# The last 64 keys of two head pairs as four 64x64 products in the array's quarters, with the work re-timed

## The chip, the cores and the metric

The kernel runs on one core of a Trainium2 chip. The metric is device time in microseconds (us) of one execution. Five engines work side by side: PE (TensorE, matmuls), ACT (ScalarE), DVE (VectorE), POOL (GpSimd, unused here but for constants) and SP (SyncE, which issues all DMAs). PE has a 128x128 array; a matmul that uses 64 of its rows or 64 of its columns leaves the other half to a second one.

## The reference

Batch 4, 12 heads, 448 positions, head size 64, model width 768, inner width 1024, all in float32.

```python
scores = scale * q @ k.T                 # per head, 448 x 448
scores = cap * tanh(scores / cap)
attn = exp(scores - max); attn /= sum(attn) + 1e-9
x = attn @ v                             # heads side by side: 448 x 768 per batch
h = relu(x @ w_in)                       # 448 x 1024
c = conv_w[0]*h[s-1] + conv_w[1]*h[s] + conv_w[2]*h[s+1]
out = (h * sigmoid(c)) @ w_out           # 448 x 768
```

## The kernel before

Heads are worked in pairs: 24 pairs p, six to a batch; the two heads of a pair stand in the lower and upper 64 partitions of `qr` and `kr`. The 448 keys of a pair are three units u of 128 keys and a rest of 64 (NU = 3, KF = 384).

**Scores** (`scores`, L420): for a unit, two matmuls with 64 contraction rows, one for each head, run side by side in the two row halves of the array, into the two banks of a PSUM tile `sp` (two such tiles, 128 x 2 x 448). The rest of both heads is one 128x128 matmul: the host lays the last 64 keys of head 0 and head 1 out in 128 columns with zeros between (`layout`, L824), so the tile `spr` has head 0 in partitions 0 to 63 and head 1 above. Pairs 0 to 11 (RAW) multiply in plain float32, which PE does in two records for each matmul; pairs 12 to 23 split q and k into a high and a low part (`qs`, `ks`, made by DVE and ACT) and use three float32r passes. ACT then does tanh and exp on each tile: on 896 columns for a unit, on 448 for the rest, into `E`.

**Values** (`values`, L463): for each of the four units, two float32 matmuls of 128 rows and 64 columns, side by side in the two column halves, add into `acc`. From pair 1 on (BUNDLE) all eight stand in one piece.

**Sums**: pairs 0 to 3 sum `E` on PE against ones (`sm`, four matmuls of 32 columns side by side). From pair 4 on DVE adds the units into a tile `P` (`add`, L489), adds the rest in two instructions on 64 partitions (`add_rest`, L497 or L494), and PE sums `P`. The reciprocals, `xu` (scaled output), and its split into `x` (high, low) follow.

**Feed forward** (`feed_forward`, L650), once a batch: `hps` (8 blocks f of 18 float32r passes), relu, three taps and the sigmoid by groups of f (0 to 2, 3 to 5, 6 and 7), the product split into `gh` and `gl`, then `ops`, 6 blocks e of 24 passes. `w_in` and `w_out` come as float64 and are decoded by ACT and DVE (`st_i`, `st_o`); the decoded `w_out` is written to DRAM (`wo`) and read back as `wh`, `wl` for each block.

The **order** on every engine comes from `Plan.run` (L85), a list planner: of the tasks that can start it takes the one with the earliest due time, counting its own costs for each engine and 0.19 us for a change of PE mode (`full`, `row`, `col`, `quad`). Due times follow from FIRST, STEP (us per pair) and DUE. The engines wait for each other by semaphores alone, so real durations set the times.

Of the kernel before, what the change touches and what calls it, by code (L numbers as in the profile page):

```python
# [20 lines left out]
TWO = 12  # L21
RAW = tuple(range(12))
STEP = (9.5,) * 8 + (17.2,) * 16
FIRST = 6.0
DUE = {"w_in": (4.4, 57.93), "w_out": (63.06, 84.72), "prep": -5.0, "load": -34.0, "av": 5.0, "sum": 4.0,
       "x": 14.0, "x0": 14.0, "one": 4.5, "rec": 2.0, "ff": 27.0, "gate": -25.0, "wq": 6.0, "wld": -15.0}
# [146 lines left out]
def capped_attention_gated_mlp_kernel(  # L173
# [17 lines left out]
    KW = KF + 128  # L191
# [183 lines left out]
    prep, b_in, t_v, b_v = {}, {}, {}, {}  # L375
# [5 lines left out]
    def prepare(p):  # L381
        b, j = divmod(p, NPB)
        t0 = when(p)
        bq, bk, bs = Buf("q"), Buf("k"), Buf("s")
        b_v[p] = Buf("v")
        ld = t0 + DUE["load"] if p else -97
        lk = dma("sp", 128 * KW * 4, lambda: new(p, raw_p, "kr", [128, KW]), lambda: k[b, j], ld, (), [bk],
                 after=t0 - AHEAD["qk"])
        lq = dma("sp", 128 * S * 4, lambda: new(p, raw_p, "qr", [128, S]), lambda: q[b, j], ld, (), [bq],
                 after=t0 - AHEAD["qk"])  # L390
        t_v[p] = dma("sp", 128 * KW * 4, lambda: new(p, raw_p, "vr", [128, KW], bufs=BUFS["v"]), lambda: v[b, j], ld + 3, (),
                     [b_v[p]], after=t0 - AHEAD["v"])
        if p in RAW:
            prep[p], b_in[p] = [lk, lq], [bq, bk]
# [12 lines left out]

        def k_hi(eng):
            copy(eng, new(p, raw_p, "ks", [128, 2, KW], F32R, bufs=BUFS["s"])[:, 0], T[p]["kr"])

        def k_lo():
            sub(T[p]["ks"][:, 1], T[p]["kr"], f32(T[p]["ks"][:, 0]))
# [3 lines left out]
        c = either(KW, k_hi, due + 0.1, [lk, a], uses=[bk, bs])  # L416
        c2 = task("dve", dve(KW), k_lo, due + 0.4, [c], uses=[bk, bs])
        prep[p], b_in[p] = [a, a2, c, c2], [bs]

    def scores(units, due):  # L420

        rest = units[0][1] == NU
        n = 1 if rest else 2
        out = [{} for _ in units]
        bufs = [Buf("m" if rest else "sp") for _ in units]

        def qk():
            for (p, u), sp in zip(units, out):
                if rest:
                    sp[0] = ps_m.tile([128, 512], F32, tag="m", name="spr").rearrange("p (a s) -> p a s", a=1)  # L430
                else:
                    sp[0] = ps_s.tile([128, 2, 512], F32, tag="sp", name="sp")
                X = T[p]
                if p in RAW:
                    parts = [(X["kr"], X["qr"])]
                else:
                    parts = [(X["ks"][:, w], X["qs"][:, l]) for w, l in ((0, 0), (0, 1), (1, 0))]
                for i, (w, x) in enumerate(parts):
                    for h in range(n):
                        r = slice(0, 128) if rest else half[h]  # L440
                        nc.tensor.matmul(out=sp[0][:, h, 0:S], lhsT=w[r, 128 * u:128 * u + 128], rhs=x[r],  # L441
                                         start=i == 0, stop=i == len(parts) - 1)

        cost = sum(2 * HALF if p in RAW else 3 * PASS for p, u in units)
        t_qk = task("pe", cost, qk, due, [t for p, u in units for t in prep[p]], bufs,
                    [b for p, u in units for b in b_in[p]], mode="full" if rest else "row")
        for (p, u), sp, bsp in zip(units, out, bufs):
            t_u = when(p, u / (NU + 1))
            raw = p in RAW
            b_e[p, u] = Buf("e")  # L450

            def tanh(sp=sp, raw=raw):
                x = sp[0][:, 0:n, 0:S]
                nc.scalar.activation(out=x, in_=x, func=ACTF.Tanh, **({"scale": tsc_sb[:, 0:1]} if raw else {}))  # L454

            def exp(p=p, u=u, sp=sp):
                E[p, u] = e_p.tile([128, 2, S], F32, tag="e", name="E")
                nc.scalar.activation(out=E[p, u][:, 0:n], in_=sp[0][:, 0:n, 0:S], func=ACTF.Exp, scale=cap_sb[:, 0:1])  # L458

            t = task("act", act(n * S, True, ptr=raw), tanh, t_u + 1, [t_qk, t_tsc], uses=[bsp])  # L460
            t_exp[p, u] = task("act", act(n * S, True, ptr=True), exp, t_u + 2, [t], [b_e[p, u]], [bsp], table="exp")

    def values(p):  # L463

        b_acc[p] = Buf("acc")

        def av(us):
            if us[0] == 0:
                T[p]["acc"] = ps_a.tile([128, 512], F32, tag="acc", name="acc")
            for u in us:  # L470
                for h in range(2):
                    c = 128 * u + 64 * h
                    nc.tensor.matmul(out=T[p]["acc"][half[h], 0:S], lhsT=T[p]["vr"][:, c:c + 64],  # L473
                                     rhs=E[p, u][:, 0 if u == NU else h, :], start=u == 0, stop=u == NU)

        for us in ([range(NU + 1)] if p >= BUNDLE else [[u] for u in range(NU + 1)]):
            t_av[p] = task("pe", 2 * HALF * len(us), lambda us=us: av(us), when(p, us[-1] / (NU + 1)) + DUE["av"],
                           [t_exp[p, u] for u in us] + [t_v[p]] + ([t_av[p]] if us[0] else []), [] if us[0] else [b_acc[p]],
                           ([b_acc[p]] if us[0] else []) + [b_v[p]] + [b_e[p, u] for u in us], mode="col")
# [3 lines left out]

# [19 lines left out]
        t_P[p] = [task("dve", dve(S), lambda h=h: add_rest(h), when(p, 0.75) + 3.5 + h, t + [t_exp[p, NU], t_eps_key],
                       uses=[b_P[p], b_e[p, NU]]) for h in range(2)]
# [273 lines left out]
    units = [(p, u) for p in range(NP) for u in range(NU)]  # L778
    while units:
        n = 2 if units[0][0] >= TWO and len(units) > 1 else 1  # L780
        scores(units[:n], when(units[0][0], units[0][1] / (NU + 1)))
        units = units[n:]
    for p in range(NP):
        scores([(p, NU)], when(p, NU / (NU + 1)))
# [15 lines left out]
def layout(inputs):  # L800
# [57 lines left out]
```

## Time and profile before

| | us |
|---|---|
| three runs | 434.56, 434.90, 435.56 |
| median | 434.9 |
| span of the profiled execution, first to last instruction | 432.9 |
| PE busy, share of the span | 418.6, 97% |
| DVE busy | 309.9, 72% |
| ACT busy | 289.1, 67% |

The page gives the profiled execution its span and no other time; the median lies 2.0 us above it, for what is around the first and the last instruction. Busy times are unions of intervals, and a matmul's interval overlaps the next one's: what a matmul costs in a stream is read from start to start. The granted clock of TensorE is at its upper level (1.00 of 2.4 GHz) in every stretch.

### The profile page before, as it was taken

The numbers are of one execution on the slowest core, as the hardware profiler recorded it, in microseconds if no ns is written. First come the engines' busy times: TensorE is split into PE (matmuls) and PEld (weight loads), VectorE is DVE, ScalarE is ACT, GpSimd is POOL, SyncE is SP. The second block draws the span as 40 slices with busy tenths as digits, with TensorE's granted clock in tenths as the row PEclk, the third lists the DMA queues.
The fourth block names the chain that finished last, engine by engine and source line by source line (L and its number), as shares of the span: only waits on it lengthen the run. The fifth ranks groups of instructions, "written<-read, shape, count | busy, mean of one in ns | idle before, by whom it ended". The sixth has DMA issues, their size and how long they took to land.

```text
span 432.9 us, 5890 instructions
## 1 busy us (share of the span) xinstructions
PE 418.6 (97%) x2106; PEld 288.1 (67%) x2106; DVE 309.9 (72%) x548; ACT 289.1 (67%) x412; POOL 0.2 (0%) x4
## 2 busy tenths in 40 slices
PE   7987889999999999999999999999999999999996
PEld 3222234457577676868667868668677787999995
DVE  1788899999999965589899773498899813166400
ACT  4999999988999665358888545368697811454411
POOL 0000000000000000000000000000000000000000
PEclk9999999999999999999999999999999999999999
DMA  7668557887556988650211762633000374500181
GB/s 273 217 225 263 182 181 234 274 244 254 206 161 200 345 292 263 229 210 5 70 28 44 224 225 90 202 130 120 24 2 0 131 251 148 183 0 2 30 336 53
DMA packets 37085, 70.90 MB, mean 164 GB/s; under 512 B 6336, under 2 KB 20160, under 8 KB 37056
## 3 DMA queue, kind: packets, MB, share of 16 engines
q1 hardware_dynamic: 37056, 70.53, 49.8%
q8 instruction: 17, 0.28, 0.3%
q14 instruction: 12, 0.10, 0.1%
HBM read 58.61 MB, written 11.84 MB: 163 GB/s over the span
## 4 chain that ended last, share of the span: by engine, by line
PE 78%; ACT 11%; DVE 7%; issue 2%; DMA 2%; ACTq 0%; DVEq 0%
PE ops L757 27%; PE hps L674 23%; PE acc L473 12%; PE sp L441 8%; ACT E L458 4%; ACT sp L454 4%; PE sm L631 2%; PE spr L441 2%; DVE P L489 1%; PE warm L280 1%; DMA kr<-in_k_dram 1%; DVE st_o L326 1%; ACT st_i L322 1%; DVE P L497 1%; DVE st_o L329 1%
## 5 line engine op out<-in xcount | busy, mean ns | idle before, releaser
L674 PE MATMUL hps<-x,wi_h 128*128 128x448 f32 x384 | 112.2, 373 | 0.0
L674 PEld LDWEIGHTS hps<-x,wi_h 128*128 128x128 f32 x384 | 70.8, 188 | 15.5 <-issue 6.7
L473 PE MATMUL acc<-E,vr 128*64 128x448 f32 x384 | 77.9, 546 | 0.0
L458 ACT ACTIVATE E<-sp,cap_sb 128x896 f32<-128x896 f32 x72 | 72.0, 1028 | 0.2
L674 PE MATMUL hps<-x,wi_l 128*128 128x448 f32 x192 | 70.2, 366 | 0.0
L700 DVE SCALAR_TENSOR_TENSOR ct<-hp,cw_sb,ct 128x448 f32<-128x448 f32 x64 | 43.1, 680 | 20.5 <-ACT ct L692 20.1
L473 PEld LDWEIGHTS acc<-E,vr 128*64 128x64 f32 x384 | 25.2, 136 | 44.3 <-issue 39.0
L636 DVE RECIPROCAL rb<-sm 128x448 f32<-128x448 f32 x12 | 35.5, 2956 | 16.4 <-PE sm L631 16.3
L757 PE MATMUL ops<-gh,wh 128*128 128x448 f32 x192 | 46.6, 372 | 0.3 <-ACT E L458 0.3
L757 PE MATMUL ops<-gh,wl 128*128 128x448 f32 x192 | 46.5, 367 | 0.0
L757 PE MATMUL ops<-gl,wh 128*128 128x448 f32 x192 | 43.8, 366 | 0.0
L441 PE MATMUL sp<-qr,kr 64*128 64x448 f32 x144 | 34.8, 582 | 8.7 <-ACT E L458 8.5
L253 ACT ACTIVATE osb<-ops 128x448 f32<-128x448 f32 x21 | 11.4, 544 | 46.6 <-PE ops L757 46.6
L757 PEld LDWEIGHTS ops<-gh,wh 128*128 128x128 f32 x192 | 35.3, 188 | 9.0 <-PE acc L473 1.4
L454 ACT ACTIVATE sp<-sp 128x896 f32<-128x896 f32 x36 | 31.0, 897 | 12.7 <-PE sp L441 12.6
L757 PEld LDWEIGHTS ops<-gh,wl 128*128 128x128 f32 x192 | 35.9, 188 | 4.1 <-DMA wh<-wo 0.7
L454 ACT ACTIVATE sp<-sp,tsc_sb 128x896 f32<-128x896 f32 x36 | 35.2, 1007 | 4.7 <-PE sp L441 4.7
L757 PEld LDWEIGHTS ops<-gl,wh 128*128 128x128 f32 x192 | 36.1, 188 | 3.1
L674 PEld LDWEIGHTS hps<-x,wi_l 128*128 128x128 f32 x192 | 36.1, 188 | 3.1
L441 PEld LDWEIGHTS sp<-qr,kr 64*128 64x128 f32 x144 | 11.8, 189 | 30.2 <-ACT E L458 18.1
L682 ACT ACTIVATE hp<-hps 128x448 f32<-128x448 f32 x32 | 17.4, 546 | 15.3 <-PE hps L674 13.0
L441 PE MATMUL sp<-qs,ks 64*128 64x448 f32 x216 | 26.9, 380 | 0.0
(84 smaller groups left out, 489.8 us busy)
## 6 DMA issues: line engine op xcount, KB each, us to landing
wh<-wo SPq DMA_DIRECT2D x24, 512.0 KB, 4.3
wl<-wo SPq DMA_DIRECT2D x24, 512.0 KB, 6.1
kr<-in_k_dram SPq DMA_DIRECT2D x24, 256.0 KB, 4.2
vr<-in_v_dram SPq DMA_DIRECT2D x24, 256.0 KB, 3.3
st_i<-in_moe_w_in_dram SPq DMA_DIRECT2D x12, 512.0 KB, 4.2
st_o<-in_moe_w_out_dram SPq DMA_DIRECT2D x24, 256.0 KB, 4.3
wo<-st_o SPq DMA_DIRECT2D x24, 256.0 KB, 3.6
qr<-in_q_dram SPq DMA_DIRECT2D x24, 224.0 KB, 4.3
```

What stands on the lines that cost most here:

```text
L253: nc.scalar.activation(out=out, in_=in_, func=ACTF.Copy)
L280: nc.tensor.matmul(out=t[:, 0:S], lhsT=ones, rhs=hp[0][:, 0:S], start=True, stop=True)
L441: nc.tensor.matmul(out=sp[0][:, h, 0:S], lhsT=w[r, 128 * u:128 * u + 128], rhs=x[r], start=i == 0, stop=i == len(parts) - 1)
L454: nc.scalar.activation(out=x, in_=x, func=ACTF.Tanh, **({"scale": tsc_sb[:, 0:1]} if raw else {}))
L458: nc.scalar.activation(out=E[p, u][:, 0:n], in_=sp[0][:, 0:n, 0:S], func=ACTF.Exp, scale=cap_sb[:, 0:1])
L473: nc.tensor.matmul(out=T[p]["acc"][half[h], 0:S], lhsT=T[p]["vr"][:, c:c + 64], rhs=E[p, u][:, 0 if u == NU else h, :], start=u == 0, stop ...
L631: nc.tensor.matmul(out=X["sm"][half[h], 0:S], lhsT=ones[:, 0:64], rhs=X["P"][:, h], start=True, stop=True)
L636: nc.vector.reciprocal(out=new(p, n_p, "rb", [128, S], bufs=BUFS["rb"]), in_=X["sm"][:, 0:S])
L674: nc.tensor.matmul(out=hps[0][:, 0:S], lhsT=w[:, c, ws], rhs=x[:, l, :], start=(c == 0 and i == 0), stop=(c == NCC - 1 and i == 2))
L682: t = task("act", act(S, True), lambda H=H, hps=hps: nc.scalar.activation(out=H[:, 1:S + 1], in_=hps[0][:, 0:S], func=ACTF.Relu), d - 10, ...
L700: nc.vector.scalar_tensor_tensor(out=ct[g][:, i], in0=H[:, o:o + S], scalar=cw_sb[:, f, o:o + 1], in1=ct[g][:, i], op0=ALU.mult, op1=ALU.add)
L757: nc.tensor.matmul(out=ops[0][:, 0:S], lhsT=W[part][:, f, :], rhs=G[l][:, f, :], start=(cnt["n"] == 0), stop=(cnt["n"] == 3 * NFC - 1))
```

## The change

Two neighbouring pairs r and r+1 share one rest. `scores` makes it a unit of its own, (r, 3): four float32 matmuls of 64 rows and 64 columns, row half by head and column half by pair, into one `sp` tile of 128 x 2 x 448 (pair r in partitions 0 to 63, r+1 above; the heads in the two banks). It is plain float32 for all pairs. ACT does one tanh and one exp on 896 columns in place of two of each on 448. `av_rest` makes four 64x64 float32 matmuls, row half by pair and column half by head, which end the sum of `acc` of pair r and begin that of r+1. DVE's `add_rest` is one instruction of 64 partitions x 896 for a pair. `k` has no zero columns any more (448 in place of 512), and `v` of an odd pair is 384 columns wide.

```diff
-STEP = (9.5,) * 8 + (17.2,) * 16
+STEP = (9.17,) * 13 + (16.34,) * 11
-DUE = {"w_in": (4.4, 57.93), "w_out": (63.06, 84.72), "prep": -5.0, "load": -34.0, "av": 5.0, "sum": 4.0,
+DUE = {"w_in": (4.4, 59.3), "w_out": (52.97, 80.43), "prep": -4.97, "load": -38.26, "av": 11.21,
...
-BIAS, SWITCH = {"act": 1.0, "dve": 1.0}, 0.1
-SLACK = {"pe": 0.0, "act": 0.1, "dve": 0.1, "sp": 0, "pool": 0}
-HOLD = 5.0
-CROSS = 0.0
+BIAS, SWITCH = {"act": 1.26, "dve": 0.91}, 0.1
+SLACK = {"pe": 0.05, "act": 0.09, "dve": 0.1, "sp": 0, "pool": 0}
+HOLD = 6.33
+CROSS = 1.4
...
+    def unit_time(p, u):
+        r = p - p % 2
+        i = u if p == r else NU + 1 + u
+        return when(r) + (when(r + 2) - when(r)) * i / (2 * NU + 1)
...
-        lk = dma("sp", 128 * KW * 4, lambda: new(p, raw_p, "kr", [128, KW]), lambda: k[b, j], ld, (), [bk],
+        vw = KF if p % 2 else VW
+        lk = dma("sp", 128 * S * 4, lambda: new(p, raw_p, "kr", [128, S]), lambda: k[b, j], ld, (), [bk],
...
-            copy(eng, new(p, raw_p, "ks", [128, 2, KW], F32R, bufs=BUFS["s"])[:, 0], T[p]["kr"])
+            copy(eng, new(p, raw_p, "ks", [128, 2, KF], F32R, bufs=BUFS["s"])[:, 0], T[p]["kr"][:, 0:KF])
...
+                sp[0] = ps_s.tile([128, 2, 512], F32, tag="sp", name="sp")
+                if u == NU:
+                    for x in of(p, u):
+                        for h in range(2):
+                            nc.tensor.matmul(out=sp[0][half[x % 2], h, 0:S], lhsT=T[x]["kr"][half[h], KF:S],
+                                             rhs=T[x]["qr"][half[h]], start=True, stop=True)
+                    continue
...
-                                     rhs=E[p, u][:, 0 if u == NU else h, :], start=u == 0, stop=u == NU)
+                    nc.tensor.matmul(out=T[p]["acc"][half[h], 0:S], lhsT=T[p]["vr"][:, c:c + 64], rhs=E[p, u][:, h, :],
+                                     start=u == 0 and not odd, stop=u == NU - 1 and odd)
+
+        def av_rest():
+            new_acc()
+            for x in (r, p):
+                for h in range(2):
+                    rows = half[x - r]
+                    nc.tensor.matmul(out=T[x]["acc"][half[h], 0:S], lhsT=T[r]["vr"][rows, KF + 64 * h:KF + 64 * h + 64],
+                                     rhs=E[r, NU][rows, h, :], start=x == p, stop=x == r)
...
-        def add_rest(h):
-            P = T[p]["P"][half[h], h]
+        def add_rest():
+            P, x = T[p]["P"][rows], E[r, NU][rows]
...
-    units = [(p, u) for p in range(NP) for u in range(NU)]
-    while units:
-        n = 2 if units[0][0] >= TWO and len(units) > 1 else 1
...
+    for r in range(0, NP, 2):
+        units = [(r, u) for u in range(NU + 1)] + [(r + 1, u) for u in range(NU)]
```

Three places show what the planner makes of it. On PE, around the second to fourth pair (`sp`, `spr`: scores; `acc`: values; `sm`: sums of the early pairs), stood before:

```order
L441 MATMUL sp<-qr,kr 128x448 x2
L441 MATMUL spr<-qr,kr 128x448
L441 MATMUL sp<-qr,kr 128x448 x4
L473 MATMUL acc<-E,vr 64x448 x8
L572 MATMUL sm<-E,ones 32x448 x8
L441 MATMUL sp<-qr,kr 128x448 x4
L441 MATMUL spr<-qr,kr 128x448
```

and now like this:

```order
L452 MATMUL sp<-qr,kr 128x448 x2
L490 MATMUL acc<-E,vr 64x448 x6
L442 MATMUL sp<-qr,kr 64x448 x4
L452 MATMUL sp<-qr,kr 128x448 x2
L490 MATMUL acc<-E,vr 64x448 x6
L604 MATMUL sm<-E,ones 32x448 x8
L452 MATMUL sp<-qr,kr 128x448 x4
L498 MATMUL acc<-E,vr 64x448 x4
```

L442 is the joint rest of the scores and L498 that of the values, once for two pairs; a value piece has six matmuls, not eight, and PE changes its mode more often.

On PE, where the first feed forward goes from `hps` to `ops` (before; `spr`, `sp` and `acc` are of pairs 10 and 11):

```order
L441 MATMUL spr<-qr,kr 128x448
L674 MATMUL hps<-x,wi_h 128x448 x2
L674 MATMUL hps<-x,wi_l 128x448
L441 MATMUL sp<-qr,kr 128x448 x4
L473 MATMUL acc<-E,vr 64x448 x8
L757 MATMUL ops<-gh,wh 128x448 x6
L757 MATMUL ops<-gl,wh 128x448 x6
L757 MATMUL ops<-gh,wl 128x448 x3
L757 MATMUL ops<-gh,wh 128x448 x2
L757 MATMUL ops<-gh,wl 128x448 x3
L757 MATMUL ops<-gl,wh 128x448 x2
```

and now, from the values and scores of later pairs through to the same passes:

```order
L789 MATMUL ops<-gh,wh 128x448 x6
L548 MATMUL sm<-P,ones 32x448 x4
L490 MATMUL acc<-E,vr 64x448 x6
L452 MATMUL sp<-qs,ks 128x448 x6
L442 MATMUL sp<-qr,kr 64x448 x4
L789 MATMUL ops<-gl,wh 128x448 x6
L789 MATMUL ops<-gh,wl 128x448 x6
L789 MATMUL ops<-gh,wh 128x448 x2
L789 MATMUL ops<-gh,wl 128x448 x2
L789 MATMUL ops<-gl,wh 128x448 x2
```

The passes x2 are the first that need `gh` and `gl` of the last two blocks f; ahead of them now stand split scores of pair 12 (`qs`, `ks`), which came after them before.

On DVE, the tile `P` of the first pair that has one (before, then now):

```order
L329 SCALAR_TENSOR_TENSOR st_i<-st_i 128x512
L251 CAST wi_h<-st_i 128x512
L489 TENSOR_TENSOR P<-P,E 128x896
L256 TENSOR_TENSOR wi_l<-st_i,wi_h 128x512
L497 TENSOR_TENSOR P<-P,E 64x448 x2
```

```order
L521 TENSOR_TENSOR P<-P,E 128x896
L257 TENSOR_TENSOR st_o<-st_o 128x256
L330 TENSOR_SCALAR st_i<-st_i 128x512
L330 TENSOR_SCALAR st_o<-st_o 128x256
L332 SCALAR_TENSOR_TENSOR st_i<-st_i 128x512
L332 SCALAR_TENSOR_TENSOR st_o<-st_o 128x256
L335 SCALAR_TENSOR_TENSOR st_i<-st_i 128x512
L528 TENSOR_TENSOR P<-P,E 64x896
```

The rest is added once for a pair, and decoding of `w_out` (`st_o`) now begins among that of `w_in` (`st_i`).

## Rows read from the trace of the kernel before

**Rows 1.** The page: busy time, then PE's busy tenths in 40 slices.

```profile
PE 418.6 (97%) x2106; PEld 288.1 (67%) x2106; DVE 309.9 (72%) x548; ACT 289.1 (67%) x412; POOL 0.2 (0%) x4
...
PE   7987889999999999999999999999999999999996
```

**Rows 2.** Busy time by stretch: PE, PEld, DVE, ACT, POOL, clock, DMA share, GB/s.

```profile
81.00:137.00 56.00, 55.54 (x269) 35.66 (x266) 54.77 (x124) 50.91 (x77) 0.00 (x0) 1.00 0.71 224
```

**Rows 3.** Waits: who waited for whom, total us, times, longest.

```profile
DVE st_i L324 <- ACT st_i L322: 11.3, 4, 8.0
...
PE sp L441 <- ACT E L458: 8.5, 8, 1.6
```

**Rows 4.** Timeline of PE, 19 to 32 us: start, us, engine, line, tiles, records.

```profile
19.21 1.02 PE L441 MATMUL sp<-qr,kr 64*128 64x448 f32 x4
20.17 1.02 PE L441 MATMUL spr<-qr,kr 128*128 128x448 f32 x2
...
24.67 3.23 PE L473 MATMUL acc<-E,vr 128*64 128x448 f32 x16
27.83 1.71 PE L572 MATMUL sm<-E,ones 128*32 128x448 f32 x16
29.47 1.77 PE L441 MATMUL sp<-qr,kr 64*128 64x448 f32 x8
31.17 1.02 PE L441 MATMUL spr<-qr,kr 128*128 128x448 f32 x2
```

**Rows 5.** Timeline of PE, 314 us.

```profile
313.97 0.77 PE L441 MATMUL spr<-qs,ks 128*128 128x448 f32 x3
314.58 0.57 PE L674 MATMUL hps<-x,wi_h 128*128 128x448 f32 x2
```

**Rows 6.** Groups by line and form: PEld, then DVE (busy us, mean ns).

```profile
L473 PEld LDWEIGHTS acc<-E,vr 128*64 128x64 f32 x384 | 25.2, 136 | 44.3 <-issue 39.0 <-ACT E L458 0.7 <-DVE st_i L324 0.7
...
L497 DVE TENSOR_TENSOR P<-P,E 64x448 f32<-64x448 f32 x16 | 9.8, 614 | 0.3
```

**Rows 7.** Timeline of ACT, 52 to 55 us, and its sigmoid near 133 us.

```profile
52.26 1.90 ACT L458 ACTIVATE E<-sp,cap_sb 128x896 f32<-128x896 f32 x2
54.04 0.62 ACT L454 ACTIVATE spr<-spr,tsc_sb 128x448 f32<-128x448 f32 x1
54.56 1.00 ACT L454 ACTIVATE sp<-sp,tsc_sb 128x896 f32<-128x896 f32 x1
...
133.33 0.95 ACT L709 ACTIVATE ct<-ct 128x896 f32<-128x896 f32 x1
```

**Rows 8.** Timeline of DVE, 136 to 139 us.

```profile
136.00 1.15 DVE L256 TENSOR_TENSOR gl<-ct,gh 128x448 fp32r<-128x448 f32 x2
137.07 0.62 DVE L552 TENSOR_TENSOR xu<-xu,rb 128x448 f32<-128x448 f32 x1
137.61 1.08 DVE L489 TENSOR_TENSOR P<-E 128x896 f32<-128x896 f32 x1
138.61 0.62 DVE L256 TENSOR_TENSOR x<-xu,x 128x448 fp32r<-128x448 f32 x1
139.14 0.68 DVE L405 SCALAR_TENSOR_TENSOR qs<-qr,tsc_sb,qs 128x448 fp32r<-128x448 f32 x1
```

**Rows 9.** Timeline of PE, 136 to 138 us and its last row.

```profile
136.20 0.57 PE L757 MATMUL ops<-gh,wh 128*128 128x448 f32 x2
...
137.22 0.58 PE L757 MATMUL ops<-gl,wh 128*128 128x448 f32 x2
...
427.63 1.79 PE L757 MATMUL ops<-gh,wl 128*128 128x448 f32 x8
```

**Rows 10.** DMA issues: queue, count, KB each, median us from issue to landing.

```profile
wl<-wo SPq DMA_DIRECT2D x24, 512.0 KB, 6.1
...
wo<-st_o SPq DMA_DIRECT2D x24, 256.0 KB, 3.6
```

More of the change, by code (lines that the diff above doesn't have):

```diff
@@ L438, in qk @@
                 for i, (w, x) in enumerate(parts):
[L439 to L441 removed]
+                    for h in range(2):
+                        nc.tensor.matmul(out=sp[0][:, h, 0:S], lhsT=w[half[h], 128 * u:128 * u + 128], rhs=x[half[h]],
                                          start=i == 0, stop=i == len(parts) - 1)
[L444 to L446 removed]
+        cost = sum(2 * HALF if p in RAW or u == NU else 3 * PASS for p, u in units)
+        modes = {"sq" if u == NU else "row" for p, u in units}
+        deps = [t for p, u in units for x in of(p, u) for t in (plain if u == NU else prep)[x]]
+        uses = [b for p, u in units for x in of(p, u) for b in (b_plain if u == NU else b_in)[x]]
+        t_qk = task("pe", cost + 0.19 * (len(modes) - 1), qk, due, deps, bufs, uses, mode=modes.pop())
         for (p, u), sp, bsp in zip(units, out, bufs):
[L448 to L449 removed]
+            t_u = unit_time(p, u)
+            raw = p in RAW or u == NU
             b_e[p, u] = Buf("e")
             def tanh(sp=sp, raw=raw):
[L453 removed]
+                x = sp[0][:, :, 0:S]
                 nc.scalar.activation(out=x, in_=x, func=ACTF.Tanh, **({"scale": tsc_sb[:, 0:1]} if raw else {}))
@@ L472, in av, with sums_of @@
                     c = 128 * u + 64 * h
-                    nc.tensor.matmul(out=T[p]["acc"][half[h], 0:S], lhsT=T[p]["vr"][:, c:c + 64],
-                                     rhs=E[p, u][:, 0 if u == NU else h, :], start=u == 0, stop=u == NU)
[L476 to L479, printed above, removed]
+                    nc.tensor.matmul(out=T[p]["acc"][half[h], 0:S], lhsT=T[p]["vr"][:, c:c + 64], rhs=E[p, u][:, h, :],
+                                     start=u == 0 and not odd, stop=u == NU - 1 and odd)
+        def av_rest():
+            new_acc()
+            for x in (r, p):
+                for h in range(2):
+                    rows = half[x - r]
+                    nc.tensor.matmul(out=T[x]["acc"][half[h], 0:S], lhsT=T[r]["vr"][rows, KF + 64 * h:KF + 64 * h + 64],
+                                     rhs=E[r, NU][rows, h, :], start=x == p, stop=x == r)
+        if odd:
+            t_av[r] = task("pe", 2 * HALF, av_rest, unit_time(r, NU) + DUE["av"] + (DUE["sq"] if p < DIRECT else DUE["sq1"]), [t_exp[r, NU], t_av[r], t_v[r]],
+                           [b_acc[p]], [b_acc[r], b_v[r], b_e[r, NU]], mode="sq")
+            t_rest[r] = t_av[p] = t_av[r]
+        for us in ([range(NU)] if p >= BUNDLE else [[u] for u in range(NU)]):
+            first = us[0] == 0 and not odd
+            t_av[p] = task("pe", 2 * HALF * len(us), lambda us=us: av(us), unit_time(p, us[-1]) + DUE["av"],
+                           [t_exp[p, u] for u in us] + [t_v[p]] + ([] if first else [t_av[p]]), [b_acc[p]] if first else [],
+                           ([] if first else [b_acc[p]]) + [b_v[p]] + [b_e[p, u] for u in us], mode="col")
+    def sums_of(p):
         if p < SUMPE:
             return
+        r, rows = p - p % 2, half[p % 2]
         b_P[p] = Buf("e")
@@ L557, in normalize_early @@
     def normalize_early(p):
-        X = T[p]
+        X, r0 = T[p], p - p % 2
+        parts = [(p, u) for u in range(NU)] + [(r0, NU)]
         due = when(p + 1)
@@ L777, in capped_attention_gated_mlp_kernel @@
         prepare(p)
-    units = [(p, u) for p in range(NP) for u in range(NU)]
-    while units:
-        n = 2 if units[0][0] >= TWO and len(units) > 1 else 1
[L781 to L784, printed above, removed]
+    for r in range(0, NP, 2):
+        units = [(r, u) for u in range(NU + 1)] + [(r + 1, u) for u in range(NU)]
+        while units:
+            n = 2 if r >= TWO and len(units) > 1 else 1
+            scores(units[:n], unit_time(*units[0]))
+            units = units[n:]
     for p in range(NP):
         values(p)
+    for p in range(NP):
+        sums_of(p)
     for p in range(SUMPE):
```

72 lines of the change are left out of this document (34 added, 38 removed).

## The prediction, made before the run

> **What bounds the kernel now.** I read the page first. PE is busy 97% of the span, and its tenths fall under 9 in the first eight slices (to some 87 us) and in the last alone [rows 1]: from there on the kernel is a stream of matmuls, and the time is what PE has to do, plus what it waits early, plus the two ends. The waits come next: the only one of size on PE is `sp` waiting for an exp of ACT, 8 times [rows 3], since there are two `sp` tiles and the next score needs one back. The third view is the stretch from 81 to 137 us: PE 55.5, DVE 54.8 and ACT 50.9 of 56 us [rows 2]. There PE has hardly a gap, but neither has DVE. Last, the timelines at 137 us: `ops` x2 at 136.20 needs the last `gh` and at 137.22 the last `gl`, and DVE's two `gl` of 1.15 us end at 137.15 [rows 8, 9]. So at 137 us DVE hands its work over just in time. I call this the gate: until it, DVE, ACT and PE all bind; behind it PE alone.
>
> **Prices on PE**, from start to start. `sp` x8 takes 29.47 to 31.17, `sp` x4 19.21 to 20.17 [rows 4]: 1.70 less 0.96 over two slots gives 0.37; I use 0.3755 for a slot, in which two float32 records run side by side, and 0.95 less 0.75 = 0.20 for the change of mode. `spr` x2, one record at a time, is two slots as well: its row lasts 1.02 like that of `sp` x4 [rows 4]. `acc` x16 takes 3.16: eight slots and 0.16. `sm` x16 takes 1.64: four slots, four records in each, and 0.14 [rows 4]. A float32r pass is 0.61 over 3 [rows 5]; I use 0.2035.
>
> **The sum over PE before.** I counted the instructions in PE's order. Ahead of the `ops` x2 at 137.22: six warm-up records (4.5), 202 float32 slots (75.9), 164 passes (33.4), 60 changes (11.0): 124.7 from PE's first matmul at 1.8, so 126.5. It came 10.7 later: the waits for ACT, and the slow first records. From there to the end: 1132 passes (230.4), 134 slots (50.3), 56 changes (10.3): 291.0. The last row starts at 427.63 and has eight passes [rows 9], so PE ends at 429.26, 292.0 behind the gate: 1.0 of waits in all that way. The copy and the store of the last block take the rest of the 432.9, 3.65.
>
> **What the change does on PE.** It removes 24 `spr` (12 of two slots, 12 of three passes: 9.0 and 7.3) and 24 value units of two slots (18.0), 34.4 in all, and adds 24 groups of four quarter products. The trace has no 64x64 product. The lower end for a group is two slots, if all four records run together, the upper four slots or more, if they don't. I take two, 0.751: two row halves run side by side (`sp`), so do two column halves (`acc`) and four column quarters (`sm`) [rows 4], and the four products take different quarters and the row halves write different banks. That adds 18.0, so PE loses 16.4 us of products. Changes of mode go the other way: 142 in the new order against 116, because the rest is a mode of its own and value pieces are cut. At 0.14 to 0.20 each that is 5.3 us back. The price of a change to and from quarters is not shown; its bounds are 0 (if a quarter counts as the mode beside it, some 4 us less) and 0.20, which I take. Net: 11.1 us less on PE.
>
> **Where it lies.** New order ahead of the `ops` x2 that needs the last `gl`: warm-up 4.5, 194 slots (72.9), 193 passes (39.3), 75 changes (13.9): 130.5, more than before, since pair 12's scores and others have been drawn ahead. Behind it: 1067 passes (217.1), 118 slots (44.3), 67 changes (12.7): 274.2, which is 16.8 less than before. So behind the gate the gain is 16.8, and the question is how much later the gate opens.
>
> **The gate.** Three engines can hold it.
> DVE: ahead of the eighth `gl` the new order has 11 more additions on 896 columns (1.00 each, 137.61 to 138.61 [rows 8]; 11.0), no more on 64x448 (14 before, 0.61 to 0.65 each by [rows 6]; 8.9 less), and more of other things: two more chains of `xu` and `x` (0.54 and 0.53 each [rows 8]; 2.1), two more copies of `xu` (1.1), pair 12's split of q and k (0.60 for the row at 139.14 [rows 8]; some 2.6 in all). With smaller ones it comes to 7.9 by the start-to-start times, 8.2 with the small gaps between DVE's instructions. The gate would be at 137.2 + 8.2 = 145.4, if DVE idles no less than the 16 us of gaps that I count in its timeline (11.3 of them waits for ACT's first step of decoding `w_in`, the longest 8.0 [rows 3]).
> ACT: a tanh or exp on 896 columns is 0.89, on 448 it is 0.52 [rows 7]. Ahead of the third sigmoid there are 20 more of 896 (17.8) and 22 fewer of 448 (11.4), and 0.5 of others: 6.9 later. It ended at 134.28 [rows 7], 2.9 ahead of the last `gl` [rows 8]; so 141.2 + 2.9 = 144.1.
> PE: 1.8 + 130.5 = 132.3, and its early waits for ACT, about what they were (it has less to do for each pair, 7.9 in place of 8.5 us, and ACT's two pairs shrink from 12.8 to 12.5 only, but passes of `hps` now fill holes from the fifth pair on): 141 to 144.
> I take 144.5, between ACT and DVE. The end is 144.5 + 274.2 + 1.0 + 3.65 = **423.3** for the span. The runs' median stands 2.0 over the span (434.9 against 432.9): **425.3**.
>
> **What costs nothing, and its cover.** The smaller loads of `k` and `v` and the moved ones have DMA at 0.71 of its engines in that stretch [rows 2] and nobody on PE waited for them; cover gone, see the third rival. ACT and DVE behind the gate have less work than before and kept up then.
>
> **Rivals.**
> *The gate opens earlier.* Where DVE's 16 us of idle time shrink (the first decoding comes 0.6 us earlier on ACT, the other three of its four waits may go, 3.3 us [rows 3]) and ACT follows, the gate is at 141: 419.8, so 421.8. For it: DVE's idle time is not needed work. Against: ACT alone gives 144.1. Chance 0.10.
> *The change doesn't bring PE time* (changes of mode and waits eat it all): they would have to take 11 us more; within 0.2% of 434.9. Against: the prices above. Chance 0.03.
> *Decoded `w_out` comes late.* By the order of DVE the decoding of the last two blocks e of `w_out` ends some 6 and 15 us later than it did, and by that of PE their passes come 0 and 14 us later. From the last decoding it takes 3.6 to write and up to 6.1 to read back [rows 10]. By my count some 6 us of margin are left for each; a wait takes their place if SP or DVE are later than that: 5 to 8 us, so 430 to 433. Chance 0.10.
> *Two quarters at a time, slower than before.* If a slot holds two records, not four, each of the 24 groups costs 0.751 more, 18.0. Thirteen lie ahead of the gate: PE arrives at 142.1 and its waits, about 149; eleven behind, 8.3. 149 + 274.2 + 8.3 + 1.0 + 3.65 = 436.2, so 438.2. It decides as soon as the groups take 9.6 us more behind and at the gate. For: no row shows quarters. Against: halves and column quarters both run side by side. Chance 0.07.
> *Weight loads that don't hide.* A load of 64 columns takes 0.136 [rows 6], and in the trace the loads of two column halves that share all rows hide: `acc` keeps 16 records in eight slots [rows 4]. If in quarters the second load of each row half showed, a group would cost 4 x 0.136 = 0.54 more; eleven behind the gate: 6.0, so 431.3. Chance 0.04. The Trainium skill, "TensorE: Matmul & The Clock Gate", Part 3 (The mechanism), says that a weight load overlaps a running matmul only if its row group differs, which speaks against products that share a row half, as these do. By that rule the time would be the 431.3 of this rival; the `acc` rows go against it.
>
> **How the numbers follow.** The forecast has 0.66: 421.5 to 429, from the gate at 141.5 to 147, a quarter's change of mode at 0 (2 us less behind the gate) and 1 or 2 us of new waits. With the earlier gate, late `w_out` and the unhidden loads inside, the range is 420.5 to 431.5; outside lie two at a time, part of the late `w_out`, and the tails. A measurement of this kernel tells about 0.2% (0.9 us) from no change. Faster: 0.66 + 0.10 + 0.10 + 0.04, less 0.01 for a late `w_out` that eats all, 0.89. Same: 0.03. Slower: two at a time and a little for what I don't see, 0.08.
>
> **What would show it.** Right: in the timeline, joint rests of eight records with about 0.95 us from start to start, change included; the last `gl` at 143 to 147 us, with PE's pieces right behind it; PE gap-free from there, 275 us to its last pass. Wrong: a group near 1.7 us (two at a time) or 1.5 (loads); PE waiting for `wh` or `wl` between 160 and 190 us; a gate beyond 149, or PE waiting at the gate for DVE while ACT idles.

## The result: 419.9 us, 14.8 us less, and the profile after

The changed kernel takes 419.91 us (median; 419.69 to 420.94) against 434.73 of the kernel before beside it: a ratio of 0.9663, 95% interval 0.9644 to 0.9682. The forecast of 425.3 had the sign right and the gain too small: 9.6 us where 14.8 came, and the time lies 0.6 us under the range. The profiled execution has a span of 417.9 us and took 419.69 in all.

The page of the changed kernel, busy time of each engine and PE's busy tenths in 40 slices, beside [rows 1]:

```profile
PE 405.9 (97%) x2142; PEld 274.2 (66%) x2142; DVE 300.7 (72%) x525; ACT 286.1 (68%) x391; POOL 0.2 (0%) x4
...
PE   6888999999999999999999999999999999999996
```

PE is busy 12.7 us less, and its tenths stay at 9 from the fifth slice on, before from the seventh (the prediction counted the first eight slices under 9; in its row it is five of the first six). To see what came from where I count, as the prediction did, PE's whole order at start-to-start prices (products and changes of mode; I call it PE's work). Prices are the prediction's; measured rows take a change into quarters at 0.16, which their own rows show (below). The span is then 1.8 to PE's first matmul, the work, the waits, and 3.67 behind the last pass:

| kernel | changes of mode | PE's work | waits | span |
|---|---|---|---|---|
| before | 116 | 415.7 | 11.7 | 432.9 |
| forecast | 142 | 404.7 | 13.1 | 423.3 |
| after | 142 | 403.7 | 8.7 | 417.9 |

"Waits" is what is left of the span; it holds real waits and stretches in which PE was slower. Of the 15.0 us between the two spans, 12.0 are work and 3.0 waits. The work came out almost as forecast. The waits are the miss: they were to grow by 1.4 us and fell by 3.0. Of that, 1.9 are waits of `sp` for exps (8.5 to 6.6 us), 0.3 is another wait for an exp, and some 0.8 the first products, which belong to the two profiled executions and not to the change (last section).

Busy time by stretch; columns as in [rows 2] (length, then PE, PEld, DVE, ACT, POOL with their instructions, granted clock, DMA share, GB/s). The kernel before, up to its hand-over at 137 us (its third stretch is [rows 2]):

```profile
12.00:45.00 33.00, 28.62 (x150) 9.07 (x150) 27.68 (x58) 32.56 (x48) 0.00 (x0) 1.00 0.68 223
45.00:81.00 36.00, 32.58 (x160) 12.34 (x158) 34.51 (x76) 34.59 (x52) 0.00 (x0) 1.00 0.69 214
```

The changed kernel, up to its own at 140.2 us and beyond:

```profile
12.00:45.00 33.00, 27.94 (x174) 8.68 (x170) 31.12 (x66) 32.38 (x44) 0.00 (x0) 1.00 0.69 225
45.00:81.00 36.00, 35.77 (x191) 12.52 (x188) 35.16 (x76) 35.87 (x52) 0.00 (x0) 1.00 0.78 245
81.00:140.20 59.20, 59.20 (x311) 37.97 (x310) 58.60 (x129) 54.63 (x79) 0.00 (x0) 1.00 0.67 206
140.20:200.00 59.80, 59.80 (x324) 44.67 (x322) 44.84 (x71) 36.99 (x55) 0.00 (x0) 1.00 0.65 222
```

From 12 us to the hand-over DVE was busy 117.0 of 125.0 us before and is busy 124.9 of 128.2 now: 7.9 more work, as forecast, but 4.7 less idle time, so the hand-over comes only 3.2 later. PE has 6.2 more work there and 3.0 less idle time; ACT 4.8 and 1.6. All three engines got denser, but not in the same place. DVE's idle time went in the first stretch above all (5.3 to 1.9), where it waited for ACT's first decoding step. That of PE grew there a little (4.4 to 5.1) and went in the second stretch (3.4 to 0.2), in which PE has 191 instructions for 160, and in the third (0.5 to 0).

The waits after, beside [rows 3] (who waited for whom, total us, times, longest):

```profile
DVE st_i L330 <- ACT st_i L328: 7.5, 4, 6.8
...
PE sp L452 <- ACT E L471: 6.6, 7, 1.4
```

PE's timeline shows how a wait goes. Before, from 53 to 69 us (start, us, engine, line, tiles, records, in brackets the idle time before it and its releaser):

```profile
53.32 1.02 PE L441 MATMUL sp<-qr,kr 64*128 64x448 f32 x4 [1.43 <-ACT E L458]
...
59.13 1.02 PE L441 MATMUL spr<-qr,kr 128*128 128x448 f32 x2
61.45 1.02 PE L441 MATMUL sp<-qr,kr 64*128 64x448 f32 x4 [1.30 <-ACT E L458]
...
68.66 0.92 PE L674 MATMUL hps<-x,wi_h 128*128 128x448 f32 x2
```

After, from 40 to 59 us:

```profile
40.17 1.02 PE L452 MATMUL sp<-qr,kr 64*128 64x448 f32 x4 [1.19 <-ACT E L471]
41.12 0.67 PE L706 MATMUL hps<-x,wi_h 128*128 128x448 f32 x2
...
54.58 0.98 PE L498 MATMUL acc<-E,vr 64*64 64x448 f32 x8
55.49 0.67 PE L706 MATMUL hps<-x,wi_h 128*128 128x448 f32 x2
56.00 0.36 PE L706 MATMUL hps<-x,wi_l 128*128 128x448 f32 x1
56.20 0.57 PE L706 MATMUL hps<-x,wi_h 128*128 128x448 f32 x2
56.61 0.36 PE L706 MATMUL hps<-x,wi_l 128*128 128x448 f32 x1
57.16 1.92 PE L452 MATMUL sp<-qr,kr 64*128 64x448 f32 x8 [0.19 <-ACT E L471]
```

Where PE waited 1.30 to 1.43 us for an exp, 1.5 us of feed-forward passes now stand, their change of mode included, and 0.19 is left. PE's first pass of `hps` (L674 before, L706 now) comes at 41.12 in place of 68.66, and behind it PE waits 0.2 us for exps in all; before, waits went on after 41 us with 1.21, 1.43 and 1.30, then 0.59 at 79 us and 0.46 at 110.

The hand-over itself, PE's timeline, beside [rows 9]:

```profile
136.62 1.48 PE L789 MATMUL ops<-gl,wh 128*128 128x448 f32 x6
...
139.78 0.57 PE L789 MATMUL ops<-gh,wl 128*128 128x448 f32 x2
140.18 0.58 PE L789 MATMUL ops<-gl,wh 128*128 128x448 f32 x2
```

and DVE's last `gl`, beside [rows 8]:

```profile
139.15 1.09 DVE L257 TENSOR_TENSOR gl<-ct,gh 128x448 fp32r<-128x448 f32 x2
```

The last `gl` ends at 140.24, the second of the two passes starts some 0.2 behind 140.18, and PE has no gap. It looks as just in time as before. Whether that means that DVE holds PE is what the experiments ask.

### The profile page after: what moved, and what is told of

Its sections match the earlier page's. It is cut to its first block, busy times and chain, and to the rows that moved or that the text cites. A ratio compares the mean times of both kernels' runs of the same rounds, so it can differ in the third digit from the quotient of the medians.

```text
span 417.9 us, 5943 instructions
## 1 busy us (share of the span) xinstructions
PE 405.9 (97%) x2142; PEld 274.2 (66%) x2142; DVE 300.7 (72%) x525; ACT 286.1 (68%) x391; POOL 0.2 (0%) x4
## 4 chain that ended last, share of the span: by engine, by line
PE 87%; ACT 10%; DVE 2%; issue 1%; ACTq 0%
PE ops L789 29%; PE hps L706 28%; PE acc L490 11%; PE sp L452 11%; ACT sp L467 4%; ACT E L471 3%; PE sm L663 2%; PE sp L442 2%; PE acc L498 2%; ACT st_i L328 1%; PE warm L286 1%; PE sm L548 1%; DVE st_i L335 0%; ACT wi_h L254 0%; DVE st_i L332 0%
## 5 line engine op out<-in xcount | busy, mean ns | idle before, releaser
L706 PE MATMUL hps<-x,wi_h 128*128 128x448 f32 x384 | 111.6, 371 | 0.0
L471 ACT ACTIVATE E<-sp,cap_sb 128x896 f32<-128x896 f32 x84 | 84.4, 1022 | 0.4
L706 PEld LDWEIGHTS hps<-x,wi_h 128*128 128x128 f32 x384 | 70.4, 188 | 19.8 <-issue 11.4
L706 PE MATMUL hps<-x,wi_l 128*128 128x448 f32 x192 | 70.2, 366 | 0.0
L490 PE MATMUL acc<-E,vr 128*64 128x448 f32 x288 | 59.5, 546 | 0.0
L467 ACT ACTIVATE sp<-sp,tsc_sb 128x896 f32<-128x896 f32 x48 | 47.3, 1000 | 4.7 <-PE sp L452 3.8
L789 PE MATMUL ops<-gl,wh 128*128 128x448 f32 x192 | 44.7, 368 | 0.0
L490 PEld LDWEIGHTS acc<-E,vr 128*64 128x64 f32 x288 | 19.0, 136 | 36.2 <-issue 33.6
L467 ACT ACTIVATE sp<-sp 128x896 f32<-128x896 f32 x36 | 31.7, 897 | 11.9 <-PE sp L452 11.9
L706 PEld LDWEIGHTS hps<-x,wi_l 128*128 128x128 f32 x192 | 36.1, 188 | 3.1
L521 DVE TENSOR_TENSOR P<-P,E 128x896 f32<-128x896 f32 x20 | 21.7, 1086 | 10.9 <-ACT E L471 10.8
L452 PEld LDWEIGHTS sp<-qr,kr 64*128 64x128 f32 x144 | 11.3, 185 | 27.5 <-ACT E L471 20.2
```

The lines of the kernel that those rows point to most:

```text
L452: nc.tensor.matmul(out=sp[0][:, h, 0:S], lhsT=w[half[h], 128 * u:128 * u + 128], rhs=x[half[h]], start=i == 0, stop=i == len(parts) - 1)
L471: nc.scalar.activation(out=E[p, u], in_=sp[0][:, :, 0:S], func=ACTF.Exp, scale=cap_sb[:, 0:1])
L521: nc.vector.tensor_tensor(out=T[p]["P"], in0=E[p, 0] if u == 1 else T[p]["P"], in1=E[p, u], op=ALU.add)
L706: nc.tensor.matmul(out=hps[0][:, 0:S], lhsT=w[:, c, ws], rhs=x[:, l, :], start=(c == 0 and i == 0), stop=(c == NCC - 1 and i == 2))
L789: nc.tensor.matmul(out=ops[0][:, 0:S], lhsT=W[part][:, f, :], rhs=G[l][:, f, :], start=(cnt["n"] == 0), stop=(cnt["n"] == 3 * NFC - 1))
```

## The experiments

The change has two halves: the quarters, and the planner's new numbers (`STEP`, `DUE` and those below them). Two accounts of its time stand against each other. By the **hold**, DVE's hand-over sets when the long stream of PE starts, and what is done for DVE or ACT ahead of it moves the end one for one. By the **balance**, PE binds all the way: the time is PE's work and its early waits, the hand-over comes when it does because PE's own passes lead to it, and taking work from DVE brings nothing. All ratios are to the kernel before, run beside each. In the expectations "theory C" is the hold and "theory D" the balance; A and B are named where they stand.

### The halves apart

**New numbers alone**, on the kernel before:

```diff
-STEP = (9.5,) * 8 + (17.2,) * 16
+STEP = (9.17,) * 13 + (16.34,) * 11
...
```

with `DUE`, `BIAS`, `SLACK`, `HOLD` and `CROSS` as in the change.

> The kernel before with the new planner numbers (STEP, DUE, BIAS, SLACK, HOLD, CROSS) and nothing else. Theory A (the products in quarters bring the gain, the numbers only order the work): PE has the same products and 116 changes of mode as before, 415.7 us by start-to-start prices; with 1.8 ahead, 3.65 behind, 2.0 around and 8 to 12 us of waits the time is 431 to 435. Rival B (the re-timing brings most of the gain, by opening the first feed forward earlier): 421 to 427.

Measured: 437.44, ratio 1.0067 (1.0050 to 1.0084), 2.9 us slower, and outside both expectations. PE's work is the same 415.7; the waits are 15.0 for 11.7. Some 1.7 of that is a lower clock behind one wait of 2.69 us (last section).

**Quarters with the old numbers**, the other half:

```diff
-STEP = (9.17,) * 13 + (16.34,) * 11
+STEP = (9.5,) * 8 + (17.2,) * 16
...
+       "x": 14.0, "x0": 14.0, "one": 4.5, "rec": 2.0, "sq": 1.88, "sq1": 4.57, "ff": 27.0, "gate": -25.0, "wq": 6.0, "wld": -15.0}
...
```

with all the other numbers of the kernel before (`sq` and `sq1`, the due times of the joint rest, didn't exist there).

> The changed kernel with the planner numbers of before (the due offsets sq and sq1, which are new, kept). Theory A: PE work is 403.7 by start-to-start prices, so 411.2 with the ends and what is around, and 9 to 13 us of waits: 420 to 424. Rival B: most of the gain is gone, 428 to 433.

Measured: 427.44, ratio 0.9834 (0.9816 to 0.9852), 7.1 us faster. PE's work is 406.2, 9.5 less than before, but with 156 changes of mode; the waits are 14.3. That lies between the two expectations, 0.6 us from rival B's. PE's first pass of `hps` comes early here too (39.54), and PE still waits: an early feed forward alone is not enough.

So the quarters bring 7.1 alone and the new numbers cost 2.9 alone, and together they bring 14.8: on the quarters the numbers are worth 7.5 us, by the profiled spans 8.1, of which 2.5 are work (14 changes of mode fewer) and 5.6 waits. The same numbers cost time on the kernel before; they suit this kernel's order.

**The old pairs' distance** on the changed kernel, and **the new distance alone** on quarters with the old numbers:

```diff
-STEP = (9.17,) * 13 + (16.34,) * 11
+STEP = (9.5,) * 8 + (17.2,) * 16
```

```diff
-STEP = (9.5,) * 8 + (17.2,) * 16
+STEP = (9.17,) * 13 + (16.34,) * 11
```

> The changed kernel with the old STEP (9.5 us for 8 pairs, then 17.2) and all other new numbers. PE's work by start-to-start prices is within 1 us of the changed kernel's. If the faster pace of the first 13 pairs is what packs the start, the time goes most of the way to the 427.4 of the old numbers: 424 to 428. If the due offsets and the bias do it, it stays at 420 to 422.

> The changed kernel with the new STEP and all other numbers old. If the faster pace alone packs the start, it is near the changed kernel: 420 to 422. If pace and offsets only work together, waits stay or grow: above the 427.4 of all old numbers, 428 to 437, with the new waits behind 57 us.

Measured: with the old distance 425.43 (0.9784, 0.9764 to 0.9804), 5.5 slower than the changed kernel: work 405.3, waits 12.2. With the new distance alone 439.36 (1.0109, 1.0087 to 1.0131), 11.9 slower than the quarters with the old numbers and above its expectation: work 404.9, waits 26.3. So the distance is worth 5.5 of the 7.5 where the other numbers go with it, and costs 11.9 where they don't; no share of the gain belongs to it alone. PE's waits with the new distance alone (columns as in [rows 3]):

```profile
PE sp L451 <- ACT E L470: 13.4, 12, 2.3
```

### Is the hand-over a hold?

**DVE less**: the joint rest's addition on 8 columns of one head for pairs 4 to 11, so the sums of those pairs leave the rest out.

```diff
-                nc.vector.tensor_tensor(out=P, in0=P, in1=x, op=ALU.add)
+                nc.vector.tensor_tensor(out=P[:, 0, 0:8], in0=P[:, 0, 0:8], in1=x[:, 0, 0:8], op=ALU.add)
```

> The changed kernel; for pairs 4 to 11 the addition of the joint rest into P touches 8 columns of one head only, in place of 896 (so these sums lack most of the last 64 keys); every order is kept. DVE has 8 x 0.9 = 7 us less ahead of the last gl of the first batch. Theory C (DVE's hand-over holds PE there): 416 to 417.5. Theory D (PE comes there with no wait, its time is its work plus the early waits for exp): 419 to 420.5, and the last gl comes some 5 us ahead of PE.

Measured: 420.01 (0.9667, 0.9647 to 0.9688), no change from 0.9663. Stretch of 81 to 140 us, then DVE's last `gl`, then PE's last pass that needs it:

```profile
81.00:140.00 59.00, 59.00 (x310) 38.11 (x310) 54.14 (x126) 55.18 (x79) 0.00 (x0) 1.00 0.66 207
```

```profile
137.87 1.09 DVE L257 TENSOR_TENSOR gl<-ct,gh 128x448 fp32r<-128x448 f32 x2
```

```profile
139.74 0.57 PE L789 MATMUL ops<-gl,wh 128*128 128x448 f32 x2
```

DVE idles 4.9 of these 59 us, and its last `gl` ends at 138.96, 0.8 ahead of PE's need, not the 5 us of the expectation: PE does not wait for it. It gets there at 139.74 in place of 140.18 and is as busy as it was. The hold would have brought the hand-over several us forward.

**The kernel before with DVE less**: its two rest additions of pairs 4 to 11 on 8 columns (their sums, too, leave the rest out).

```diff
-                nc.vector.tensor_tensor(out=P, in0=P, in1=E[p, NU][half[h], 0], op=ALU.add)
+                nc.vector.tensor_tensor(out=P[:, 0:8], in0=P[:, 0:8], in1=E[p, NU][half[h], 0, 0:8], op=ALU.add)
```

> The kernel before; for pairs 4 to 11 the two additions of the rest into P touch 8 columns in place of 448 (these sums lack most of the last 64 keys); every order is kept. DVE has 16 x 0.55 = 9 us less, 7.7 of them ahead of its hand-over at 137 us. Theory C as the prediction had it (the hand-over held PE at 137 us): 429 to 432. Theory D (PE came there without a wait): 434 to 435.5, and the last gl ends some 5 us ahead of PE's use.

Measured: 433.77 (0.9976, 0.9964 to 0.9987), 1.0 us faster. DVE's last `gl` and PE's use:

```profile
135.13 1.16 DVE L256 TENSOR_TENSOR gl<-ct,gh 128x448 fp32r<-128x448 f32 x2
```

```profile
136.36 0.57 PE L757 MATMUL ops<-gl,wh 128*128 128x448 f32 x2
```

I took some 7.7 us of work from DVE and the last `gl` moved from 137.15 to 136.29, 0.9. The time lies between the two expectations, near that of the balance, and the 5 us ahead didn't come here either. From 12 to 137 us DVE is busy 112.4 us for 117.0 and idles 12.6 for 8.0. So in the kernel before, on which the prediction's argument rests, DVE's amount of work was not the hold either: it waits for the others in between.

**DVE more**: eight instructions on 896 columns added for the same pairs (a maximum of two tiles).

```diff
+                nc.vector.tensor_tensor(out=T[p]["P"], in0=T[p]["P"], in1=E[r, NU], op=ALU.max)
```

> The changed kernel with one more instruction on 896 columns for each of pairs 4 to 11 on DVE (a maximum of P with the joint rest's E, which changes these sums); every order is kept. 8 x 1.0 = 8 us more on DVE ahead of the last gl of the first batch. Theory C: all of it shows, 427 to 428. Theory D: what exceeds DVE's slack shows; with no slack at all 427 to 428 too, with a slack of 3 to 5 us 423 to 425. With the run of less DVE work the two tell a balance (less brings nothing, more costs) from a gate (both show).

Measured: 429.36 (0.9880, 0.9865 to 0.9896), 9.4 slower than the changed kernel for 8.1 us of work (1.01 each from start to start). PE's timeline at the hand-over, then ACT's and DVE's:

```profile
130.98 0.98 PE L498 MATMUL acc<-E,vr 64*64 64x448 f32 x8
135.19 1.08 PE L790 MATMUL ops<-gh,wh 128*128 128x448 f32 x4 [3.23 <-ACT hp L715]
```

```profile
134.59 0.55 ACT L715 ACTIVATE hp<-hps 128x448 f32<-128x448 f32 x1 [3.43 <-DVE ct L748]
```

```profile
132.01 1.09 DVE L529 TENSOR_TENSOR P<-P,E 128x896 f32<-128x896 f32 x1
...
133.88 1.69 DVE L748 TENSOR_TENSOR ct<-ct,hp 128x448 f32<-128x448 f32 x3
```

and the stretches there (columns as in [rows 2]):

```profile
131.00:136.00 5.00, 1.77 (x14) 0.93 (x13) 4.97 (x9) 1.57 (x5) 0.00 (x0) 1.00 0.18 44
136.00:140.00 4.00, 4.00 (x14) 3.47 (x13) 4.00 (x13) 3.97 (x7) 0.00 (x0) 0.59 0.00 0
```

Now DVE does hold PE, through ACT: PE waits 3.2 us for ACT to take `hp` out of its tile, ACT 3.4 for DVE's multiply `ct`, and DVE is busy 4.97 of 5 us with work ahead of it, an added instruction (L529) among it. PE's other named waits grow by 2.6 (1.3 for `P`, 1.3 for exps). And the granted clock then is 0.59 for 4 us, 1.6 us lost; the rest of the 10.0 that the waits grew isn't named. So DVE has no room upward, though taking work away brings nothing: at 58.6 of 59.2 us it is level with PE, not ahead of it.

**ACT less**: tanh of the six joint rests below pair 12 on 8 columns of each head, so there the scores are not capped.

```diff
-                x = sp[0][:, :, 0:S]
+                x = sp[0][:, :, 0:S] if u < NU or p >= 12 else sp[0][:, :, 0:8]
...
-                                     scale=cap_sb[:, 0:1])
+                                     scale=cap_sb[:, 0:1] if u < NU or p >= 12 else tsc_sb[:, 0:1])
```

> The changed kernel; the tanh of the six joint rests of pairs 0 to 11 works on 8 columns of each head in place of 448 (left out on the others, and their exp has another scale); every order is kept. ACT has 6 x 0.65 = 3.9 us less, about half of it ahead of 57 us, where all of PE's waits for exp lie. Theory D (the time is PE's work plus these early waits): 1 to 2.5 us less, 417.5 to 419. Theory C (DVE's hand-over at 140 us holds): unchanged, 419.5 to 420.5.

Measured: 419.55 (0.9645, 0.9629 to 0.9662), not told apart from 0.9663. PE's waits for exps fall from 6.6 to 5.9, so the 1 to 2.5 us that the balance expected of ACT didn't come. The amount of ACT's work doesn't hold the time either; what sets the exps that PE waits for is not shown by this run.

### Does PE's work count, early and late?

**Joint scores three times, late** (pairs 12 to 23) **and early** (pairs 0 to 11): 48 more products of quarters each, 12 groups of 0.751, 9.0 us of PE; the values are the same.

```diff
-                    for x in of(p, u):
+                    for x in of(p, u) * (3 if p >= 12 else 1):
```

```diff
-                    for x in of(p, u):
+                    for x in of(p, u) * (3 if p < 12 else 1):
```

> The changed kernel; the four score products of each joint rest of pairs 12 to 23 are issued three times (the same result); every order is kept. 12 groups of two slots more, 9.0 us of PE, five of the six rests behind the hand-over at 140 us. Theory D and theory C alike: all of it shows where PE alone binds, 428 to 429.5. If less than 6 shows, PE has hidden waits there.

> The same for pairs 0 to 11: 9.0 us more of PE work ahead of 140 us; every order is kept. Theory D: what lies beside PE's waits for exp (three rests ahead of 57 us, waits of 0.7 to 1.5 us near them) may be hidden, 3 to 4 us at most, the rest shows: 424.5 to 429. Theory C: PE has slack ahead of the hand-over, nothing or little shows: 419.5 to 422.

Measured: late 429.11 (0.9866, 0.9847 to 0.9886), 9.2 more; early 427.53 (0.9829, 0.9812 to 0.9845), 7.6 more. Late, every us counts. Early, 1.4 lies beside waits. PE's waits in the early one:

```profile
PE sp L452 <- ACT E L471: 5.4, 4, 1.5
```

By the hold, early work would have been taken up by PE's idle time ahead of the hand-over and shown little or nothing; 7.6 of 9.0 show.

### Another set of numbers

**The changed kernel with other planner numbers**, to see whether its own are the end:

```diff
-STEP = (9.17,) * 13 + (16.34,) * 11
+STEP = (7.35,) * 19 + (17.83,) * 5
...
-DUE = {"w_in": (4.4, 59.3), "w_out": (52.97, 80.43), "prep": -4.97, "load": -38.26, "av": 11.21,
+DUE = {"w_in": (9.41, 58.2), "w_out": (50.9, 71.87), "prep": -4.58, "load": -21.46, "av": 7.43,
...
```

(and the rest of that block).

> The changed kernel with another set of planner numbers, in which the first 19 pairs go at 7.35 us and the last five at 17.83. PE has the same products, 136 changes of mode in place of 142 (1.1 us less by their prices), and if the waits ahead of 60 us shrink by 1 to 2 us as well: 416.5 to 419. If the denser start makes DVE late, as the run with more DVE work was: 421 to 425.

Measured: 419.15 (418.49 to 422.45), ratio 0.9645 (0.9629 to 0.9661), which the intervals don't tell from the 0.9663 of the change. It has 1.1 us less work (402.6, 136 changes of mode). The execution in its profile is the slowest of the six, 422.45, and there the waits are 12.6:

```profile
55.00:58.00 3.00, 1.29 (x7) 0.84 (x5) 1.97 (x6) 3.00 (x4) 0.00 (x0) 1.00 0.65 199
58.00:62.00 4.00, 3.73 (x10) 1.33 (x12) 3.66 (x7) 2.79 (x5) 0.00 (x0) 0.57 0.81 243
```

PE waits 1.98 us for an exp before 58.27, and then has a clock of 0.57 for 4 us: 1.7 us. It also waits 1.5 us for a decoded block (`wh`). What its other runs did there isn't shown.

## Why the prediction was right and wrong

**Prices on PE: right.** Products fell by 16.4 as counted. PE's timeline of joint rests after (start, us, records):

```profile
11.26 1.08 PE L442 MATMUL sp<-qr,kr 64*64 64x448 f32 x8
12.27 0.97 PE L490 MATMUL acc<-E,vr 128*64 128x448 f32 x4
...
21.32 0.98 PE L498 MATMUL acc<-E,vr 64*64 64x448 f32 x8
```

From start to start, with the change of mode into them, eight records take 1.01 us in this first group and 0.91 in most (54.58 to 55.49 above; 18 of the 21 groups behind which PE doesn't wait), where I said about 0.95. Two slots are 0.751, so four 64x64 records do run together. The change into a group is then 0.16 in most, not the 0.20 that I took: 24 x 0.04, 1.0 us less work. That is the whole of 404.7 against 403.7.

**Two at a time; loads that don't hide: refuted.** The first needs 1.7 us for a group and the second 1.5. The loads, by line and form (busy us, mean ns, idle before):

```profile
L442 PEld LDWEIGHTS sp<-qr,kr 64*64 64x64 f32 x96 | 2.7, 131 | 5.8 <-issue 2.6 <-ACT E L471 1.6 <-ACT x L254 0.7
L498 PEld LDWEIGHTS acc<-E,vr 64*64 64x64 f32 x96 | 2.5, 131 | 5.4 <-issue 5.4
```

A load takes 131 ns, and a group that showed one for each of its products would be 0.5 us longer than these are. The rule of the Trainium skill, "TensorE: Matmul & The Clock Gate", Part 3 (The mechanism), that a load overlaps only a matmul in another row group (the section also names a load into the background weight buffer, which no run here can tell apart), is not borne out here as it stands: `av_rest` (L498) works two heads, one right behind the other, on the same rows, and its groups take 0.91 us (54.58 to 55.49 in the timeline of the changed kernel above).

**Late `w_out`: didn't come.** PE is busy 59.80 of 59.80 us from 140.2 to 200 (the windows above), so what it saves behind the hand-over is kept: from 140.18 to the end it takes 277.7, where the sum had 274.2 + 1.0 + 3.65 = 278.85. Of these 1.1 us, 0.4 are the quarters' cheaper changes and 0.7 waits that I had put in.

**The gate: the step that failed.** It said 144.5, between ACT's 144.1 and DVE's 145.4; it was 140.2, 4.3 earlier, of which 0.5 is again the price of the changes. The prediction's words were "if DVE idles no less than the 16 us of gaps that I count in its timeline", and of PE's early waits "about what they were". Each of the three terms took the engine's own added work (DVE's is right to 0.3 us; ACT's, up to the end of the third sigmoid at 137.46, is 5.6 for the 6.9 forecast) and left its idle time as it was, as though idle time were part of what has to be done. It isn't: up to the hand-over DVE idles 4.7 us less, PE 3.0 and ACT 1.6. DVE's went for the most part where it waited for ACT's decoding (11.3 to 7.5 us of waits), ahead of PE's first `hps`; PE's went where passes of `hps` stand in its waits; that they are the cause is read from the timeline, not tested by a run of its own. So the hand-over came just under PE's own term: 1.8, 130.0 of work and 8.4 of waits are 140.2, where that term had 130.5 of work, 8.7 to 11.7 of waits and so 141 to 144, and the prediction went by the later terms of ACT and DVE. The rival "the gate opens earlier" was this, at 0.10 and with 141 us; its 421.8 is 1.9 over the time that came, 0.8 of it at the gate and 1.1 behind. I held ACT's 144.1 against it, which was the same mistake once more.

Behind it stands a misreading of [rows 8, 9]. That the last `gl` ends within 0.1 us of PE's use was taken for a hold. Less work on DVE moved it by 0.9 in the kernel before and by 1.3 in the changed one (140.24 to 138.96), and the time by 1.0 and by nothing. A just-in-time hand-over is what an order with no slack on either side looks like; it doesn't say which side sets it. The sum against the span closes: 423.3, less 1.0 (price of quarters), less 4.4 (waits 8.7, not 13.1), is 417.9.

What isn't settled is why this order has 8.7 us of waits and others have 12 to 26. That the numbers only work together is shown (three mixes of old and new are 5.5 to 19.5 us slower than the change), and that it is waits more than work; which of the due times lets the passes come at the right moment wasn't tried one by one, nor was the early `hps` tried by itself.

## What to carry to other kernels

An engine's idle time ahead of a hand-over is not a constant to carry into the new sum: bound the hand-over by the busy times alone on one side and by busy times with the old idle time on the other, and keep both in the range. Before you call a just-in-time hand-over a hold, ask what the waiting side would do if it came earlier; a run with some work taken from the supposed holder, and one with some added, tells (0 and +9.4 us here). Numbers that set an order are worth what they are worth with the instructions they were found for: the same block cost 2.9 us on one kernel and brought 7.5 on the other.

## What the runs showed of the hardware

**The clock after a wait.** In the kernel before, the granted clock is 1.00 in every stretch shown, with single waits of PE for exps up to 1.58 us. After waits of 1.98 (other numbers), 3.23 (DVE more) and 2.69 us (new numbers alone) it was 0.57 to 0.67 over the next 4 us: for most of them the lower of TensorE's two levels, 1.2 in place of 2.4 GHz. The third of these, busy by stretch:

```profile
59.00:60.00 1.00, 0.01 (x2) 0.01 (x2) 1.00 (x5) 1.00 (x3) 0.00 (x0) 1.00 0.10 14
60.00:64.00 4.00, 4.00 (x14) 1.32 (x16) 3.94 (x8) 4.00 (x8) 0.00 (x0) 0.67 0.51 150
```

PE is busy without a gap from 60 to 64 us, at a clock a third lower; with 0.81 over the next 2 us that is 1.7 us lost. With the new distance alone, after waits of 2.34 and 0.97, it was 0.50 for 5 us and 0.56 for 2 more, 3.4 us lost in all. But a wait of 2.33 us in that same run, up to 80.41, left it at 1.00:

```profile
80.00:84.00 4.00, 3.59 (x20) 1.23 (x24) 3.49 (x6) 3.64 (x6) 0.00 (x0) 1.00 0.89 292
```

So a single wait of 2 to 3 us cost some 1.7 us more than it lasted in three runs and nothing more in one place, and part of what I call waits in those runs is this. In the profiles of the kernel before and of the change the clock is 1.00 throughout their waits.

**The first products.** The first `sp` x8 after the warm-up took 2.22 us in the profile of the kernel before (6.58 to 8.74 from start to start) and 1.77 in that of the changed one, though both do the same there:

```profile
6.58 2.22 PE L441 MATMUL sp<-qr,kr 64*128 64x448 f32 x8
```

```profile
6.21 1.77 PE L452 MATMUL sp<-qr,kr 64*128 64x448 f32 x8
```

With the warm-up records ahead of them that is some 0.8 us of the 15.0 between the two profiles. It belongs to the execution and not to the change: with ACT less, in the changed kernel's order, the first `sp` starts at 6.58 again and takes 2.44.
